# Four row blocks instead of two column halves: w_out's load and the order of batch 1's second layer in an attention and GELU kernel

## The chip, the core and the metric

The kernel runs on one core of a Trainium2 chip. Its time is the device time of one execution in microseconds; the number compared is the median of several runs. One further execution is recorded by the hardware profiler, and all rows below are from it. PE is TensorE, DVE is VectorE, ACT is ScalarE, POOL is GpSimd and SP is SyncE, which here only issues DMAs.

## What is computed

For 8 batches, 12 heads, 448 positions and a head width of 64, the reference normalizes q and k, computes attention, and puts the joined heads through two dense layers with a tanh GELU between them:

```python
q_n, k_n = rmsnorm(q, g_q), rmsnorm(k, g_k)
scores = (1 / sqrt(64)) * q_n @ k_n.T
attn = softmax(scores) @ v                          # 8 x 12 x 448 x 64
x = attn.transpose(0, 2, 1, 3).reshape(3584, 768)
h = x @ w_in                                        # 768 x 2048
out = gelu_tanh(h) @ w_out                          # 2048 x 768, out is 3584 x 768
```

Inputs and output are float32.

## The kernel before

The matmuls are in bf16. Batches are numbered from 0. The work is a pipeline over them: while the attention of batch b + 1 runs, the second layer of batch b is fed between its pieces. Everything is placed by hand. Each engine runs its instructions in the order in which the program emits them, and each queue issues its DMAs in that order too, so an instruction that waits holds up whatever was emitted behind it on its engine.

**Attention.** The 12 heads are three groups c = 0, 1, 2 of four heads. Within a group a `unit` (L321) is one of seven blocks t of keys: four PE matmuls of kT and qT into PSUM, then one exponential on ACT. `key_sums` (L340) adds the exponentials on DVE into `es`; `products` (L365) multiplies them by ones (sums) or V on PE; `turned` and `recips` make reciprocals on DVE, and `quad_x` writes xT, the first layer's input.

`attention` (L497) goes through eight groups of two or three units. Before each group the `side` steps of that number are emitted, after it the `behind` steps; in between a set number of second-layer steps are taken from the list `m2`, 20 in the first group of batch 1's attention and 13 in each of the next two, 96 in all.

**The second layer.** A step `mm2` (L432) is one matmul of 128 positions by 384 of w_out's 768 columns, for one block f of 128 of the 2048 hidden features. Sixteen steps, f = 0 to 15, fill one half of an output tile; then DVE, or ACT from the fourth group on in batch 1's attention, copies it into `osb`. After half 1 SP stores the whole tile in two DMAs. `m2_parts` (L482) lists the steps. The list made for b = 0 holds tiles 0 to 2 and runs during batch 1's attention; that is what the diff's title means by batch 1's second layer. It is sorted there by halves: half 0 of the three tiles, then half 1 of the three.

**Loads.** q and k are loaded by SP (`loads`; `late_loads` writes one element with DVE first, which holds the load until DVE has got there). Weights and V are loaded by POOL, which also squares and normalizes; these DMAs turn float32 into bf16 on the way. `w_in_part` loads half of w_in in four DMAs, `w_out_part` half of w_out's columns in one. They stand in the long step 8 of `mid` (L726), in this order: the second half of w_in, squares of batch 1's group 0, w_out half 0, batch 1's V, squares of group 1, w_out half 1.

**kT of group 1.** In batch 1's preparation kT and qT of groups 0 and 2 are transposed on PE, those of group 1 by DMA on SP (`dma_trans`, L308). `gain` (L316) then multiplies kT by the gains on DVE, emitted in group 1 of batch 1's attention ahead of that group's DVE work. The first unit that reads this kT is the second of the three in group 2. In the same two `side` groups batch 2's q and k are loaded (`late_loads` of its groups 0, then 1 and 2); POOL squares groups 0 and 1 and DVE sums the squares in `behind` of group 4.

Of the kernel before, what the change touches and what calls it, by code (L numbers as in the profile page):

```python
# [17 lines left out]
def kernel(  # L18
# [23 lines left out]
    HP = H // 2  # L42
    nf = d_ff // 128
    HD = d_model // 2
# [61 lines left out]
    wout = wts.tile([128, nf, d_model], BF16)  # L106
# [36 lines left out]
    def load_v(b, i, n):  # L143

        nc.gpsimd.dma_start(
            vb[b % 2][:, i:i + n].rearrange("p a t d -> p a (t d)"),
            v[b, 2 * i:2 * (i + n)].rearrange("(a r) (p t) d -> (r p) a (t d)", r=2, t=NT),
        )
# [6 lines left out]
    def square(b, c, n, eng, hs=both, ts=slice(0, NT)):  # L155
        if (n, b, c) not in sqs:
            sqs[n, b, c] = sqp.tile([P, 2, NT, D], F32, tag="sq", name="sq")
        sq, raw = squares(b, c, n, hs, ts), raws[n, b, c][:, hs, ts]
        if eng is nc.scalar:
            nc.scalar.activation(sq, raw, AF.Square)  # L160
        else:
            eng.tensor_mul(sq, raw, raw)  # L162
# [97 lines left out]
    def idle(n, w):  # L260

        for _ in range(n):
            nc.tensor.matmul(w, zeros[:, :128], zeros, start=True, stop=True)
# [168 lines left out]
    def mm2(b, i, half, f, lo, hi):  # L432

        end = b + 1 == B and i + 1 == 2 * S // 128
        if f == 0:
            osbs["ps"] = ps_m.tile([128, 512], F32, tag="mm", name="o")
            if lo == 0:
                osbs[i] = op.tile([128, d_model], F32, tag="osb", name="osb")
        o, osb = osbs["ps"][:, :hi - lo], osbs[i]
        nc.tensor.matmul(  # L440
            o, g[:, f, i * 128:(i + 1) * 128], wout[:, f, lo:hi],
            start=(f == 0), stop=(f == nf - 1),
        )
        if f + 1 < nf:
            return
        last = end and hi == d_model
        if b + 1 == B and (lo == 0 or end) or by_act:
            nc.scalar.copy(osb[:, lo:hi], o)  # L448
        else:
            nc.vector.tensor_copy(osb[:, lo:hi], o)  # L450
        if half == 0 and not end:
            return
        for j in range(2):
            col = i * 128 + j * R
            r = ((b // 2) * 2 + col // S) * R
            cols = slice(lo if end else 0, hi)
            eng = nc.scalar if last and j else nc.sync
            eng.dma_start(
                out_v[col % S // R, r:r + R, cols], osb[j * R:(j + 1) * R, cols]
            )  # L460
# [21 lines left out]
    def m2_parts(b):  # L482
        tiles = range(3) if b % 2 == 0 else range(3, 7)
        order = [(i, half) for i in tiles for half in range(2)]
        if b == 0:

            order.sort(key=lambda t: t[1])
        parts = [(i, half, half * HD, (half + 1) * HD) for i, half in order]
        if b + 1 == B:
            i, half, lo, hi = parts.pop()  # L490
            parts += [(i, half, lo, lo + HD // 2), (i, half, lo + HD // 2, hi)]
        return [
            lambda part=part, f=f: mm2(b, part[0], part[1], f, *part[2:])
            for part in parts for f in range(nf)
        ]
# [146 lines left out]

    def w_out_part(i):
        nc.gpsimd.dma_start(
            wout[:, :, i * HD:(i + 1) * HD],
            moe_w_out[:, i * HD:(i + 1) * HD].rearrange("(f p) d -> p f d", p=128),
        )

    def warm():
        return oall[0][:, :S]  # L650
# [57 lines left out]
    for a in range(2):  # L708
# [20 lines left out]
            lambda: normed(0, 2, "k", nc.vector, t_rest), lambda: recips(),  # L729
            lambda: w_in_part(1, 2),  # L730
            lambda: square(1, 0, "q", nc.gpsimd), lambda: square(1, 0, "k", nc.gpsimd),
            lambda: w_out_part(0), lambda: load_v(1, 0, HP),
            lambda: square(1, 1, "q", nc.gpsimd), lambda: square(1, 1, "k", nc.gpsimd),
            lambda: w_out_part(1)),
           (9, lambda: idle(2, warm())),
           (10, lambda: products(0, 0, 1, 0, 3)),
           (11, lambda: products(0, 0, 1, 3)),
# [24 lines left out]
    for b in range(B):  # L762
# [50 lines left out]
        for f in range(nf // 2 if b == 0 else nf):  # L813
# [7 lines left out]
            for fn in m1.get(f, ()):  # L821
                fn()
        m2 += m2_parts(b)
        if b + 1 == B:
            for fn in m2:
# [44 lines left out]
```

## Time and profile before

| | us |
|---|---|
| runs | 407.31, 406.19, 407.34; median 407.31 |
| profiled execution, time | 408.13 |
| its span | 406.4 |
| PE busy | 395.6 |
| ACT busy | 280.8 |
| DVE busy | 258.1 |
| POOL busy | 121.3 |
| w_out half 0, half 1: issued | 28.14, 33.47 |
| batch 1's V: issued | 29.36 |
| first second-layer matmul | 54.3 |

The span is the time from the first to the last instruction; the profiled execution's time is 1.7 us more. Times within the execution count from the start of the span. The second layer takes 912 matmuls of PE's 3331. The granted clock is 1.0 throughout.

### The profile page before, as it was taken

The page shows a single profiled execution, that of the slowest core. Times are in us where ns is not written, and L with a number is a line of the kernel's source. Part 1 is how long each engine was busy: PE and PEld are TensorE (multiplying, and loading weights), DVE is VectorE, ACT ScalarE, POOL GpSimd, SP SyncE. Part 2 cuts the span into 40 slices and gives each one's busy share as a digit, 9 for nine tenths or more (in the row PEclk, how much of TensorE's full clock was granted, in tenths as well). Part 3 has the DMA queues.
Part 4 walks back from the last instruction along what each step waited for, and adds up shares of the span by engine and source line. Part 5 has one row for each costly group of instructions (what it writes and reads, how often), then busy time and mean ns, then how long its engine had stood idle before and what let it go on. Part 6 is the DMA issues. An engine that isn't in the chain of part 4 may idle for free.

```text
span 406.4 us, 8105 instructions
## 1 busy us (share of the span) xinstructions
PE 395.6 (97%) x3331; PEld 209.4 (52%) x3331; DVE 258.1 (64%) x433; ACT 280.8 (69%) x380; POOL 121.3 (30%) x101
## 2 busy tenths in 40 slices
PE   7799999999999999999999999999999999999996
PEld 3354555555555555555555555555555555555564
DVE  4988956986698258945689357973598504990010
ACT  5995388967974888847976689748878349754301
POOL 4994307265005440092203640073300900000000
PEclk9999999999999999999999999999999999999999
DMA  8999996989613936159622939139713511111033
GB/s 268 322 209 207 200 188 230 233 192 260 107 40 86 271 54 185 39 123 286 122 65 48 235 82 227 43 73 255 98 40 80 111 27 39 42 48 31 1 78 78
DMA packets 65561, 54.07 MB, mean 133 GB/s; under 512 B 37364, under 2 KB 60532, under 8 KB 65524
## 3 DMA queue, kind: packets, MB, share of 16 engines
q1 hardware_dynamic: 53184, 41.48, 39.2%
q0 software_dynamic: 12112, 11.80, 18.7%
q8 instruction: 26, 0.43, 0.4%
q10 hardware_dynamic: 228, 0.28, 0.2%
q14 instruction: 11, 0.09, 0.1%
HBM read 45.61 MB, written 11.01 MB: 139 GB/s over the span
## 4 chain that ended last, share of the span: by engine, by line
PE 89%; DVE 3%; POOL 2%; DMA 2%; ACT 1%; issue 1%; SPq 0%; DVEq 0%; POOLq 0%
PE o L440 36%; PE h L419 23%; PE t L470 12%; PE t L330 9%; PE t L381 8%; DMA rawq<-in_q_dram 2%; ACT ex L334 1%; POOL g L162 1%; DVE st L390 1%; PE tp L288 1%; DVE rb L397 1%; POOL win L641 0%; DVE es L352 0%; DVE ss L167 0%; POOL sq L162 0%
## 5 line engine op out<-in xcount | busy, mean ns | idle before, releaser
L334 ACT ACTIVATE ex<-t,shift 128x896 bf16<-128x896 f32 x168 | 157.8, 1006 | 22.6 <-PE t L330 19.9
L440 PE MATMUL o<-wout,g 128*128 128x384 bf16 (+1 forms) x912 | 156.8, 324 | 0.0
L440 PEld LDWEIGHTS <-g 128*128 128x128 bf16 x912 | 83.6, 98 | 67.9 <-issue 18.9
L419 PE MATMUL h<-xT,win 128*128 128x448 bf16 x504 | 96.5, 352 | 0.0
L167 DVE TENSOR_REDUCE ss<-sq 128x14 f32<-128x896 f32 (+3 forms) x45 | 44.4, 1000 | 50.6 <-ACT sq L160 46.7
L419 PEld LDWEIGHTS <-win 128*128 128x128 bf16 x504 | 49.3, 98 | 46.0
L425 ACT ACTIVATE g<-h 128x448 bf16<-128x448 f32 x84 | 45.7, 544 | 28.1 <-PE h L419 23.0
L450 DVE COPY osb<-o 128x384 f32<-128x384 f32 x41 | 22.7, 554 | 52.4 <-PE o L440 50.5
L470 PE MATMUL t<-xT,win 128*128 128x448 bf16 x264 | 51.6, 352 | 0.1
L330 PE MATMUL t<-qT,kT 64*64 64x448 bf16 x672 | 47.0, 359 | 2.4 <-DVE kT L297 1.0
L475 ACT ACTIVATE g<-t 128x896 bf16<-128x896 f32 x22 | 19.4, 915 | 34.8 <-PE t L470 33.5
L654 POOL COPY mark<-es 1x1 bf16<-1x1 bf16 x6 | 1.1, 178 | 132.7 <-DVE es L352 132.7
L270 POOL TENSOR_TENSOR nrmq<-rawq,rinv 128x896 bf16<-128x896 f32 (+1 forms) x21 | 34.8, 1659 | 11.5 <-DVE o L233 7.3
L470 PEld LDWEIGHTS <-win 128*128 128x128 bf16 x264 | 25.7, 98 | 24.0 <-issue 0.8
L270 POOL TENSOR_TENSOR nrmk<-rawk,rinv 128x896 bf16<-128x896 f32 x19 | 31.9, 1681 | 0.0
L381 PE MATMUL t<-ex,vb 64*64 64x448 bf16 x588 | 31.6, 350 | 0.0
L330 PEld LDWEIGHTS <-kT 64*64 64x64 bf16 x672 | 17.2, 105 | 27.4 <-issue 20.3
L448 ACT COPY osb<-o 128x384 f32<-128x384 f32 (+1 forms) x16 | 7.3, 459 | 31.7 <-PE o L440 31.7
L162 POOL TENSOR_TENSOR sq<-rawq 128x896 f32<-128x896 f32 (+1 forms) x9 | 13.6, 1517 | 50.1 <-DVE ss L167 31.8
L397 DVE STREAM_TRANSPOSE rb<-rc 128x896 f32<-128x896 f32 x24 | 26.7, 1112 | 0.8
L390 DVE STREAM_TRANSPOSE st<-t 128x448 f32<-128x448 f32 x42 | 24.6, 625 | 3.2 <-PE t L381 3.1
L381 PEld LDWEIGHTS <-vb 64*64 64x64 bf16 x672 | 19.9, 107 | 12.4 <-issue 3.0
(89 smaller groups left out, 302.5 us busy)
## 6 DMA issues: line engine op xcount, KB each, us to landing
out_dram<-osb SPq DMA_DIRECT2D x54, 192.0 KB, 2.7
rawq<-in_q_dram SPq DMA_DIRECT2D x23, 448.0 KB, 4.6
rawk<-in_k_dram SPq DMA_DIRECT2D x23, 448.0 KB, 5.7
vb<-in_v_dram POOLq DMA_DIRECT2D x7, 672.0 KB, 6.7
win<-in_moe_w_in_dram POOLq DMA_DIRECT2D x8, 384.0 KB, 12.7
wout<-in_moe_w_out_dram POOLq DMA_DIRECT2D x2, 1536.0 KB, 23.9
vb<-in_v_dram POOLq DMA_DIRECT2D x1, 448.0 KB, 10.5
qT<-nrmq SPq DMA_TRANSPOSE x19, 5.0
```

Source lines behind the costliest of these rows:

```text
L167: nc.vector.reduce_sum(sss[b][:, c, "qk".index(n), hs, ts], squares(b, c, n, hs, ts), axis=AX.X)
L270: eng.tensor_mul(nrms[n, b, c][:, ts].rearrange("p t a d -> p a t d"), raws[n, b, c][:, :, ts], root[:, :, ts].to_broadcast([P, 2, m, D]),)
L330: nc.tensor.matmul(sc[r * R:(r + 1) * R, a, :S], kT[rs, c, t, r], qT[b][rs, c, :, r], start=True, stop=True,)
L334: nc.scalar.activation(ex[:, t], sc[:, :, :S], AF.Exp, scale=scale, bias=shift)
L381: nc.tensor.matmul(o[r][a * D:(a + 1) * D], vb[b % 2][rs, 2 * c + a, i] if what else ones[rs], es[i][rs, a], start=(i == 0), stop=(i == n ...
L390: nc.vector.transpose(st[:, r].rearrange("p a b -> p (a b)"), oas[0][r])
L397: nc.vector.transpose(rb.rearrange("p r s -> p (r s)"), rc.to_broadcast([128, 2 * S // 32, 32]))
L419: nc.tensor.matmul(h[:, :S], win[:, c, f * 128:(f + 1) * 128], xT[b][:, c], start=(c == 0), stop=(c == HP - 1),)
L425: nc.scalar.activation(g[:, f, (b % 2) * S:(b % 2 + 1) * S], h[:, :S], AF.Gelu_apprx_tanh)
L440: nc.tensor.matmul(o, g[:, f, i * 128:(i + 1) * 128], wout[:, f, lo:hi], start=(f == 0), stop=(f == nf - 1),)
L450: nc.vector.tensor_copy(osb[:, lo:hi], o)
L470: nc.tensor.matmul(h[:, j, :S], win[:, c, f * 128:(f + 1) * 128], xT[b][:, c], start=(c == 0), stop=(c == HP - 1),)
```

## The change

The two w_out loads, each of 2048 rows by 384 columns (rows of 1536 bytes in float32), become four loads of 512 rows by all 768 columns (3072 bytes). In the feature blocks that a matmul reads, load i holds f = 4i to 4i + 3, for both column halves. Two of them now stand ahead of the squares of group 1 and two behind them, and batch 1's V comes last. The sort by halves goes, so the list for b = 0 is tile 0 half 0, tile 0 half 1, tile 1 half 0 and so on, as for the other batches.

```diff
     def m2_parts(b):
         tiles = range(3) if b % 2 == 0 else range(3, 7)
         order = [(i, half) for i in tiles for half in range(2)]
-        if b == 0:
-
-            order.sort(key=lambda t: t[1])
...
     def w_out_part(i):
         nc.gpsimd.dma_start(
-            wout[:, :, i * HD:(i + 1) * HD],
-            moe_w_out[:, i * HD:(i + 1) * HD].rearrange("(f p) d -> p f d", p=128),
+            wout[:, 4 * i:4 * (i + 1)],
+            moe_w_out[512 * i:512 * (i + 1)].rearrange("(f p) d -> p f d", p=128),
         )
...
             lambda: w_in_part(1, 2),
             lambda: square(1, 0, "q", nc.gpsimd), lambda: square(1, 0, "k", nc.gpsimd),
-            lambda: w_out_part(0), lambda: load_v(1, 0, HP),
+            lambda: w_out_part(0), lambda: w_out_part(1),
             lambda: square(1, 1, "q", nc.gpsimd), lambda: square(1, 1, "k", nc.gpsimd),
-            lambda: w_out_part(1)),
+            lambda: w_out_part(2), lambda: w_out_part(3), lambda: load_v(1, 0, HP)),
```

## The prediction

> **What bounds the kernel now.** I read the page first (TensorE, PE, is busy 97% of the span), then the windows, to see whether it idles anywhere the change can reach. The columns of a row are PE, weight loads, DVE, ACT and POOL.
>
> ```profile
> 54.00:62.00 8.00, 8.00 (x70) 4.29 (x63) 4.39 (x14) 7.76 (x9) 0.00 (x0) 1.00 1.05 209
> 62.00:70.00 8.00, 8.00 (x95) 3.94 (x93) 4.74 (x7) 6.69 (x8) 6.47 (x6) 1.00 0.74 253
> 70.00:76.00 6.00, 6.00 (x70) 3.09 (x68) 5.84 (x12) 5.16 (x8) 1.29 (x2) 1.00 0.75 106
> 76.00:82.00 6.00, 6.00 (x83) 3.38 (x81) 5.40 (x10) 5.94 (x10) 2.93 (x3) 1.00 0.90 294
> ```
>
> The four rows cover batch 1's attention, in which the edited second layer runs. PE is full in all of them, and the later rows lose 0.16 us between 100 and 380. So no wait is there to be removed, and any wait put in front of PE after 54 us is added whole. The clock is 1.00 throughout.
>
> Next the landings, from the DMA view of narrow stretches; the last number is us from issue to landing.
>
> ```profile
> win<-in_moe_w_in_dram POOLq DMA_DIRECT2D x1, 384.0 KB, 16.2
> ...
> wout<-in_moe_w_out_dram POOLq DMA_DIRECT2D x1, 1536.0 KB, 19.6
> vb<-in_v_dram POOLq DMA_DIRECT2D x1, 672.0 KB, 22.7
> ...
> wout<-in_moe_w_out_dram POOLq DMA_DIRECT2D x1, 1536.0 KB, 28.2
> ...
> kT<-nrmk SPq DMA_TRANSPOSE x1, 13.4
> ```
>
> With the issue times of the timeline (24.22, 28.14, 29.36, 33.47, 45.34) they land at 40.4, 47.7, 52.1, 61.7 and 58.7: POOL's DMAs land in order of issue, one after the other. Half 0 of w_out is needed at 54.3 and half 1 at about 64.9, so neither is waited for now.
>
> Then the packets of both queues, in 40:42, 48:50 and 54:56 (q0 is POOL's queue, q1 SP's with the DMA transposes):
>
> ```profile
> q0 software_dynamic: 521, 0.40, 130.6%
> ...
> q0 software_dynamic: 374, 0.29, 91.5%
> q1 hardware_dynamic: 367, 0.09, 35.8%
> ...
> q0 software_dynamic: 372, 0.29, 90.7%
> q1 hardware_dynamic: 368, 0.09, 35.6%
> ```
>
> Alone, q0 moves 521 packets of 768 bytes in 2 us. Beside the transposes (256-byte packets) the two queues take turns one packet each, whatever the sizes. Last, the timeline around the place where kT lands:
>
> ```profile
> 54.27 3.42 PE L440 MATMUL o<-wout,g 128*128 128x384 bf16 x20
> 58.72 0.45 DVE L317 TENSOR_SCALAR kT<-kT,gcols 128x896 bf16<-128x896 bf16 x1 [0.55 <-DMA kT<-nrmk]
> 60.54 0.76 PE L330 MATMUL t<-qT,kT 64*64 64x448 bf16 x12
> 61.03 0.55 DVE L450 COPY osb<-o 128x384 f32<-128x384 f32 x1
> 61.64 0.37 SPq L122 DMA_DIRECT2D rawq<-in_q_dram  x1
> 77.66 1.35 DVE L352 TENSOR_TENSOR es<-es,ex 128x896 bf16<-128x896 bf16 x2
> 79.08 0.37 PE L381 MATMUL t<-es,ones 64*64 64x448 bf16 x4
> ```
>
> DVE already waits 0.55 us for kT, 2 us before PE reads it (the second of the three units at 60.54, so 60.8). At the end es is ready at 79.01 and read at 79.08: no slack there.
>
> **The change part by part.** The 96 second-layer steps, their evictions and the switch of evictions to ACT (a matter of the count alone) are the same: 0.
>
> *Issues on POOL.* A w_out half (2048 rows) takes 1.22 us, a part of w_in (192) 0.63: 0.32 us per 1000 rows, so a block of 512 is 0.73. Four are 2.93 instead of 2.43, hidden by POOL's idle 7.30 us before 41.98. The squares of (1, 1) start about 0.6 us earlier. V's issue goes from 29.36 to about 34.4; V is read at 66.3 and must land with the queue's end, about 61: 0.
>
> *The last w_out block.* V took 52.1 - 47.7 = 4.3 us in the queue and now comes last, so at an unchanged end w_out would be complete at 61.7 - 4.3 = 57.4. Three things make it earlier. Packets of 1536 bytes: from 61 ns at 768 (2 us x 16 engines / 521) and 157 ns at 2048 (204 in 30:32), 119 ns by interpolation, 3 ns saved on each of 128 per engine, 0.4. Transposes that have not yet got their turn: some 48 of 112 packets per engine, at 86 - 61 = 25 ns, 1.2. Batch 2's q loads, which shared the last 2.5 us before: about 0.9. So 54.9 to 57.4. The first tile reads block 3 at its 13th matmul, 54.34 + 12 x 0.168 = 56.4. PE waits 0 to 1.0; I take 0.3.
>
> *kT.* The two transposes, of qT and kT, move 458,752 bytes, 1792 packets or 112 per engine, each behind one of q0. Beside w_out a turn goes from 86 ns (32 us of 16 engines / 370) to 119 + 25 = 144 ns. Their first packets move at about 47.6 (DMA view in narrow windows). On an engine that began w_out at 37 (in 36:38 most packets are already of the small kind), 128 x 0.119 ends at 52.2 without them, with them at 53.2; 39 turns are done, 48 follow beside V at 91 ns (32 / 352), 25 alone, with the 0.4 us in which all packets stop near 53: kT lands at about 59.2. On the last engine (w_in's last landing is 40.4) the same sum ends at 61.8 and lands by 62.2. A landing is that of the last of 16 engines, so I stay near the upper end, and take the old end of all this traffic, 61.7, less the 0.4 saved: 61.2. The gain then ends at 61.7 instead of 59.2, and PE, which wants it at 60.8, waits 0.9 in all (the 0.3 above falls inside).
>
> The Trainium skill, "DMA: Bandwidth & Descriptors", section "Queues, rings and completion order", has engines alternate between queues by packets of typically 9 to 17 descriptors. The nearly equal counts above speak for one traced packet a turn. If turns were of about equal bytes, kT would still land at 58.7 and this term were 0.
>
> *What waits behind that gain.* On DVE: three additions, then the eviction that completes tile 0. That goes from 61.03 to about 63.5. SP now has tile 0's two stores (0.56 us each, from the pair at 107.44) ahead of batch 2's loads; with the halves those stores came at 74.1. So the loads go at about 65.2 instead of 61.64, 3.6 later. POOL's squares of (2, 1) end at 74.1 instead of 70.46. DVE's last reduction of them would start at 72.5 + 0.9 = 73.4: 0.7 late. DVE is packed from there to the es of 79.01, so PE waits 0.7 more. Without the late kT the stores cost 1.1 on SP, inside the 2.0 us of slack (72.5 - 70.46): 0.
>
> *Stores.* Two tiles leave earlier, out of SP's train of 9.28 us at 74.11. The next transposes wait for POOL's norms too, and PE is full from 82 to 100 (18.00 of 18.00): 0.
>
> Sum: 0.9 + 0.7 = +1.6, from 408.1 to 409.7 of the profiled execution. That one is 0.8 above the median of 407.3, so the median becomes 408.9. With kT at 62.7 the PE wait is 2.4 and the sum 3.1; with kT at 59.2 and block 3 at 56 it is 0.
>
> **The rivals.**
> 1. *All hidden.* The last engine catches up, or turns are by bytes; kT lands before 60.2. For it: 1.5 to 2 us of slack; an average engine is done at 59.2. Against: the 3.4 us by which the last engine trails. 407.3.
> 2. *Each smaller load costs a gap.* If every load pays about 2 us before the next moves, two more loads put w_out's end at 57 + 4 = 61, and PE waits 4.4 at its 13th matmul: 411.7. Against: the w_in parts land 1.6 to 2.4 us apart and are 393 KB each, about 200 GB/s, the rate of the long halves. The fixed 2.0 us per DMA are those of the Trainium skill, same page, section "Anatomy of one DMA — SWDGE (gpsimd) path"; this trace shows no such gap.
> 3. *Faster.* POOL squares 0.6 us earlier and leaves DVE alone sooner, while DVE makes the xT for which PE idles. It decides if the transposes and products at 30.4 to 36 become shorter. PE's idle time from 28 to 38 is 0.85 us (1.82, 1.47 and 1.86 busy of 2.00 in three rows), which with the 0.16 later bounds the gain at 1.0: 406.3. Against: DVE's pair of transposes takes 1.17 to 1.18 us beside POOL and without it.
>
> **How the numbers follow.** About 0.3% (1.2 us) is what a measurement of this kernel tells from no change. Forecast 0.60, of which 0.08 stays within 1.2 us; hidden 0.22; gap 0.10; faster 0.08, of which 0.05 passes the bound with the spread of the runs (406.19 to 407.34) and 0.03 does not. Slower 0.52 + 0.10 = 0.62; same 0.08 + 0.22 + 0.03 = 0.33; faster 0.05. The range takes in the hidden case with its spread, 406.6, and the forecast's upper cost 3.1 with half of the gap case, 411.2.
>
> **What would show it.** Right: DVE's idle time before the gain of kT grows from 0.55 to about 3 us, PE shows a wait of about 1 us at 60 to 62, batch 2's second loads are issued after 64 and tile 0's stores ahead of them. w_out's blocks land near 44, 48, 52 and 56. Wrong: PE still full from 54 to 82, or kT landed before 60; packets of q0 and q1 no longer equal in number while both run; or PE's wait at the 13th matmul is the larger one.

## The result and the profile after

The changed kernel takes 409.43 us (median of 20 runs, 407.44 to 411.89) against 406.81 (20 runs, 406.17 to 407.83) before: a ratio of 1.0067 [1.0053, 1.0081], or 2.6 us more. Its runs spread over 4.45 us, those of the kernel before over 1.66. The profiled execution took 408.96 us with a span of 407.2.

First the windows, on the same stretches as for the kernel before. The columns are PE, weight loads, DVE, ACT and POOL, then granted clock, DMA share and GB/s.

```profile
54.00:62.00 8.00, 7.72 (x65) 4.03 (x62) 2.88 (x8) 7.76 (x9) 0.00 (x0) 1.00 0.93 137
62.00:70.00 8.00, 8.00 (x95) 3.92 (x93) 5.76 (x13) 6.21 (x8) 3.54 (x3) 1.00 0.81 239
70.00:76.00 6.00, 5.64 (x67) 2.83 (x64) 5.42 (x12) 5.16 (x7) 4.21 (x5) 1.00 0.50 136
76.00:82.00 6.00, 6.00 (x84) 3.48 (x81) 5.53 (x9) 5.94 (x9) 2.12 (x3) 1.00 1.16 275
```

PE, full before in all four, now lacks 0.28 us in the first row and 0.36 in the third. DVE does 1.5 us less work in the first row (2.88 against 4.39) and 1.0 more in the second, and POOL's squares have moved from the second row (6.47 to 3.54) into the third (1.29 to 4.21). From the first matmul of L470 after this stretch (81.39 before, 82.19 after) to the end of the span both kernels take the same time, about 325.0 us. So the cost arises ahead of it.

The two queues in 48:50 and the landing of kT, from the DMA view:

```profile
q0 software_dynamic: 224, 0.34, 93.8%
q1 hardware_dynamic: 224, 0.06, 21.7%
...
kT<-nrmk SPq DMA_TRANSPOSE x1, 15.3
```

The two queues are still equal in packets, 224 each instead of 374 and 367. POOL's queue moves more bytes (0.34 MB instead of 0.29) and the transposes fewer (0.06 instead of 0.09). kT was issued at 45.02 and lands at 60.3. The blocks of w_out land at 42.7, 46.5, 50.8 and 55.4, V at 59.9. Now the timeline behind that landing:

```profile
60.37 0.45 DVE L317 TENSOR_SCALAR kT<-kT,gcols 128x896 bf16<-128x896 bf16 x1 [2.52 <-DMA kT<-nrmk]
60.88 0.57 PE L330 MATMUL t<-qT,kT 64*64 64x448 bf16 x8 [0.28 <-DVE kT L317]
62.66 0.55 DVE L450 COPY osb<-o 128x384 f32<-128x384 f32 x1
63.24 1.19 SPq L458 DMA_DIRECT2D out_dram<-osb  x2
64.52 0.55 SPq L122 DMA_DIRECT2D rawq<-in_q_dram  x1
69.78 1.83 POOL L162 TENSOR_TENSOR sq<-rawq 128x448 f32<-128x448 f32 x2 [3.48 <-DVE xT L405]
73.42 0.62 DVE L167 TENSOR_REDUCE ss<-sq 128x7 f32<-128x448 f32 x1 [0.27 <-POOL sq L162]
74.51 1.17 DVE L390 STREAM_TRANSPOSE st<-t 128x448 f32<-128x448 f32 x2
75.74 0.38 PE L330 MATMUL t<-qT,kT 64*64 64x448 bf16 x4 [0.36 <-DVE st L390]
```

Read it downwards. DVE idles 2.52 us for kT, and PE waits 0.28 for DVE's gain. The eviction of tile 0 comes at 62.66, its two stores go out, and only then q of batch 2's group 1 is issued, at 64.52 (before at 61.64). POOL starts its squares at 69.78 (before at 66.85), and though the row names xT as what ended the idle time, the q they need lands at 69.6, 5.1 us after the issue. DVE's sums of those squares, the last at 73.42, stand ahead of the transposition `st` of 74.51. That instruction empties the PSUM buffer which the last unit of group 5 writes to, and so PE waits a second time, 0.36 us at 75.74. In the kernel before, the same two places read as follows, and PE's twelve matmuls go through without a break:

```profile
73.70 1.18 DVE L390 STREAM_TRANSPOSE st<-t 128x448 f32<-128x448 f32 x2
74.66 0.76 PE L330 MATMUL t<-qT,kT 64*64 64x448 bf16 x12
```

### The profile page after: what moved, and what is told of

The parts are those of the page before. It is cut to its first block, busy times and chain, and to the rows that moved or that the text cites. A ratio compares the mean times of both kernels' runs of the same rounds, so it can differ in the third digit from the quotient of the medians.

```text
span 407.2 us, 8108 instructions
## 1 busy us (share of the span) xinstructions
PE 396.1 (97%) x3331; PEld 209.4 (51%) x3331; DVE 258.1 (63%) x433; ACT 280.8 (69%) x380; POOL 122.0 (30%) x103
## 4 chain that ended last, share of the span: by engine, by line
PE 81%; DVE 6%; DMA 6%; POOL 3%; issue 2%; ACT 1%; SPq 1%; DVEq 0%; POOLq 0%
PE o L440 33%; PE h L419 23%; PE t L470 8%; PE t L330 8%; PE t L381 7%; DMA kT<-nrmk 4%; DMA rawq<-in_q_dram 2%; DVE ss L167 1%; DVE st L390 1%; POOL sq L162 1%; PE o L381 1%; POOL g L162 1%; DVE rb L397 1%; DVE xT L410 1%; DVE es L352 0%
## 5 line engine op out<-in xcount | busy, mean ns | idle before, releaser
L167 DVE TENSOR_REDUCE ss<-sq 128x14 f32<-128x896 f32 (+3 forms) x45 | 44.6, 1000 | 50.8 <-ACT sq L160 45.9
L470 PE MATMUL t<-xT,win 128*128 128x448 bf16 x264 | 51.6, 352 | 0.1
L470 PEld LDWEIGHTS <-win 128*128 128x128 bf16 x264 | 25.7, 98 | 24.0 <-issue 0.8
```

The lines of the kernel that those rows point to most:

```text
L167: nc.vector.reduce_sum(sss[b][:, c, "qk".index(n), hs, ts], squares(b, c, n, hs, ts), axis=AX.X)
L470: nc.tensor.matmul(h[:, j, :S], win[:, c, f * 128:(f + 1) * 128], xT[b][:, c], start=(c == 0), stop=(c == HP - 1),)
```

## The experiments

Two theories for the size of the cost. One: the late kT alone makes it, by holding DVE and with it everything behind. The other: the stores, which now stand on SP ahead of batch 2's loads, must be there too. Beside them stood the rivals of the prediction. In the table, the first three columns come from timed runs, with the median of the kernel before on the same chip; the last five from the profiled execution: the first second-layer matmul, PE's waits for w_out, for group 1's kT or qT, and for `st`, and what is left of the time after that first matmul, less the 353.86 us that this is before (408.13 - 54.27). Each row has one profile, and the timed runs of a kernel spread around it.

| kernel | median (before) | ratio [95%] | start | w_out | kT, qT | `st` | cost |
|---|---|---|---|---|---|---|---|
| whole change, first profile | 409.43 (406.81) | 1.0067 [1.0053, 1.0081] | 53.95 | 0 | 0.28 | 0.36 | 1.15 |
| whole_again | 409.79 (407.03) | 1.0066 [1.0044, 1.0088] | 52.48 | 0 | 0.31 | 1.99 | 2.90 |
| whole_look | profile alone, 408.50 | | 53.05 | 0 | 0.35 | 0.78 | 1.59 |
| whole_look_2 | profile alone, 408.07 | | 53.56 | 0 | 0 | 0.36 | 0.65 |
| whole_look_3 | profile alone, 412.80 | | 54.14 | 0.38 | 1.52 | 2.14 | 4.80 |
| loads_only | 408.18 (406.47) | 1.0037 [1.0021, 1.0054] | 52.43 | 0 | 1.58 | 0 | 1.85 |
| order_only | 413.27 (406.47) | 1.0174 [1.0151, 1.0196] | 52.74 | 3.47 | 0 | 0 | 6.32 |
| v_last | 406.81 (406.47) | 1.0010 [0.9997, 1.0023] | 52.35 | 0 | 0 | 0 | 0.00 |
| v_late | 408.01 (406.47) | 1.0040 [1.0024, 1.0056] | 54.02 | 0.64 | 0 | 0 | 0.55 |
| loads_ahead | 407.85 (407.03) | 1.0019 [1.0002, 1.0036] | 53.81 | 0 | 0.36 | 0 | 0.53 |
| k_first | 407.55 (407.03) | 1.0009 [0.9987, 1.0031] | 54.12 | 0 | 0.84 | 0 | 0.64 |
| stores_behind | 408.42 (406.59) | 1.0030 [1.0012, 1.0049] | 53.39 | 0.22 | 1.54 | 0 | 2.24 |
| k_first_loads_ahead | 408.04 (406.59) | 1.0021 [1.0004, 1.0039] | 52.47 | 1.40 | 0.09 | 0 | 1.47 |

The start varies by 1.7 us between the five executions of the whole change, but in every profile, that of before included, it comes 26.13 or 26.14 us after the issue of the first w_out load. What moves it lies before the first edited instruction, and the last column leaves it out.

**Each half of the change alone.** loads_only keeps the new loads and puts the sort back; order_only takes the sort out and keeps the old loads.

```diff
 # loads_only: the four blocks, V last, and in m2_parts again
+        if b == 0:
+            order.sort(key=lambda t: t[1])
 # order_only: no sort, w_out by column halves, V behind half 0
```

> The four row blocks with V last, but the second layer still by halves (the order of before). Theory 1 (kT of group 1 is late because the transposes take turns with packets twice as large; the late gain and, behind it, tile 0's stores ahead of batch 2's loads make PE wait): kT lands at 59.5 to 62 as after the whole change, DVE's idle time before the gain is 2 us or more, PE waits for it, but SP issues batch 2's second loads at about 63, right behind their DVE writes, without the stores, so the second wait (DVE's sums behind POOL's squares, 0.4 to 0.7 us) is gone. Time 0.5 to 2 us above before, less than the 2.6 of the whole change. Theory 2 (the order by tiles is the cost: the stores stand ahead of the loads, the late kT is within its slack): time as before within 0.5 us. Theory 3 (w_out itself lands late for the tile order): as before, since half 1 is then read only from 64.9.

> The second layer tile by tile, with the loads of before (two column halves, V between them). Half 1 of w_out lands at about 61.7 and is now read at the 17th matmul, 54.3 + 16 x 0.168 = 57.0. Both theories 1 and 3: PE waits 4.7 us there for the DMA of w_out, kT lands at about 58.7 inside that wait and costs nothing of its own; time 4 to 5.5 us above before. Theory 2 (order by stores alone): about 2.6 us above, as with the whole change, with no PE wait at the 17th matmul.

loads_only costs 0.37%, a little over half of the whole. Its DMA view of 48:50, and PE's wait in its timeline:

```profile
q0 software_dynamic: 227, 0.34, 93.9%
q1 hardware_dynamic: 224, 0.06, 21.6%
...
kT<-nrmk SPq DMA_TRANSPOSE x1, 16.6
```

```profile
60.66 0.57 PE L330 MATMUL t<-qT,kT 64*64 64x448 bf16 x8 [1.58 <-DVE kT L317]
```

kT lands 16.6 us after its issue, at 60.1, and that one wait, 1.58 us, is most of its cost of 1.85. There is no second wait. So the new loads alone make kT late, and the new order adds something else.

order_only cost more than twice what the whole change does, 6.8 us by the medians, above the 4 to 5.5 expected. From its timeline, and its windows:

```profile
58.98 1.46 PE L440 MATMUL o<-wout,g 128*128 128x384 bf16 x4 [3.47 <-DMA wout<-in_moe_w_out_dram]
```

```profile
55.00:59.00 4.00, 0.53 (x5) 0.12 (x3) 1.55 (x5) 1.41 (x2) 0.00 (x0) 0.84 1.11 201
59.00:61.00 2.00, 2.00 (x12) 0.77 (x16) 0.00 (x0) 0.00 (x0) 0.11 (x1) 0.50 0.82 265
```

The 17th matmul, the first of half 1, waits 3.47 us for the second load. Then the granted clock falls to 0.50; it is 0.50 until 63 and 0.61 from 63 to 65, and thirteen second-layer matmuls take 3.71 us instead of 2.29. PE is busy throughout these six microseconds, so the low clock loses 1.0 + 1.0 + 0.8 us of work there; with the wait that is 6.3, the cost of this profile (6.32). The waits of up to 2.14 us in whole_look_3 left it at 1.00. The Trainium skill, "TensorE: Matmul & The Clock Gate", section "What's actually happening", has the clock fall to half after an idle window of about 3.4 us; this trace agrees, with 3.47 us. So the sort by halves was what hid the second load before; in tile order with column halves it is waited for.

**V moved, the packets kept.** v_last takes the kernel before and moves one issue only.

```diff
-            lambda: w_out_part(0), lambda: load_v(1, 0, HP),
+            lambda: w_out_part(0),
             lambda: square(1, 1, "q", nc.gpsimd), lambda: square(1, 1, "k", nc.gpsimd),
-            lambda: w_out_part(1)),
+            lambda: w_out_part(1), lambda: load_v(1, 0, HP)),
```

> Before with one move alone: batch 1's V issued behind w_out half 1; column halves (packets of 768 bytes) and the order by halves stay. It differs from the run with row blocks and order by halves only in the size of w_out's packets and the place of two issues. Theory 1 (turns by packet): the transposes still pass one for each 768-byte packet, at some 86 ns a turn, and kT lands at 58.2 to 59, as before; no PE wait; time as before within 0.4 us. Rival (kT is late because V now stands last in the queue and the queue as a whole ends at 60 to 61, whatever the packets): kT lands at 60 to 61 and the time is 0.5 to 2 us above before, equal to the row blocks with order by halves.

The ratio's interval includes 1, and PE shows no wait. This profile and that of loads_only start alike, at 52.35 and 52.43, so they compare directly. From the DMA views of v_last, the packets in 48:50 and kT's line in 46:48, and then its gain:

```profile
q0 software_dynamic: 372, 0.29, 90.7%
q1 hardware_dynamic: 372, 0.10, 36.0%
...
kT<-nrmk SPq DMA_TRANSPOSE x1, 13.2
```

```profile
56.61 0.45 DVE L317 TENSOR_SCALAR kT<-kT,gcols 128x896 bf16<-128x896 bf16 x1 [0.37 <-DMA kT<-nrmk]
```

The queue ends at the same time in both (V lands at 60.1 here, at 59.9 in loads_only), with the same bytes in the same order of weights and V. Yet kT lands at 56.6 with packets of 768 bytes and at 60.1 with those of 1536. The counts of the two queues are equal in both, 372 to 372 and 227 to 224, while the bytes are not. What delays kT is neither V's place nor the end of the queue, but the size of the packets that it takes turns with. (The two kernels also differ in the number of w_out loads, four for two, and by 0.7 us in the issue of V; no run separates these from the size.)

**V taken out of the competition.** v_late is the whole change, but POOL issues V only when batch 1's first sums of exponentials are there, at about 57.7.

```diff
-            lambda: w_out_part(2), lambda: w_out_part(3), lambda: load_v(1, 0, HP)),
+            lambda: w_out_part(2), lambda: w_out_part(3)),
...
-            side += [(1, lambda: late_loads(2, 0), lambda: gain(1, 1)),
+            side += [(1, lambda: gpsimd_waits(ess[1, 0][:1, 0, :1]), lambda: load_v(1, 0, HP),
+                      lambda: late_loads(2, 0), lambda: gain(1, 1)),
```

> The whole change, but batch 1's V is issued by POOL only when batch 1's first key sums are there (about 57), so that the transposes of group 1 meet w_out's packets and nothing after them. Theory 1: the transposes run alone once w_out has landed (55.4 on the last engine) and kT lands at 56.5 to 58.5, before DVE gets to the gain or shortly after; PE waits for it no more; stores cost 1.1 us on SP inside the slack; V lands at about 64.5, before 66.5, when it is read. Time as before within 0.6 us, that is some 2 us below the whole change, and the spread of its runs falls from 4.5 us towards that of before, 1.7. Theory 2 (stores ahead of loads): time as with the whole change, 2 to 2.6 us above before. If V comes too late (after 66.5) PE waits there for it, and the time says nothing of kT.

DVE no longer idles ahead of the gain (58.13), and PE's only wait is 0.64 us for w_out's last block, at its 13th second-layer matmul. So in this profile a kT in time takes both later waits away. At 1.0040 it still isn't as fast as before: its median is 1.5 us above, where 0.6 was expected and the profile costs 0.55. The late last block is one candidate for the rest. V is another: it lands at 66.5, and its first weights are read at 66.7, so a slightly later V would be waited for. Which of them it is in the timed runs is not shown.

**The whole change again, and batch 2's loads put first.** loads_ahead moves the loads of batch 2's groups 1 and 2 one step earlier on SP and DVE, ahead of the gain and of tile 0's stores.

```diff
-            side += [(1, lambda: late_loads(2, 0), lambda: gain(1, 1)),
-                     (2, lambda: late_loads(2, 1), lambda: late_loads(2, 2))]
+            side += [(1, lambda: late_loads(2, 0), lambda: late_loads(2, 1),
+                      lambda: late_loads(2, 2), lambda: gain(1, 1))]
```

> The whole change once more, for a second profile. In the runs so far kT lands at 57 to 60 by the DMA stream, while the first second-layer matmul starts anywhere from 52.3 to 54.3, so the profiled run of the change (53.95) would be one in which PE came late. Theory 1: with a start near 52.4 PE waits 1.5 to 2 us for the gain of kT, its time is then 409 to 410; with a start near 54 it waits 0.3. In both, POOL's squares of (2, 1) end late and DVE and then PE wait 0.4 to 1 more. Theory 2 (only the stores ahead of the loads cost): no wait for kT however early PE is.

> The whole change, with batch 2's second and third q and k loads (and the DVE writes that hold them) moved ahead of the gain of kT, so neither the gain nor tile 0's stores stand before them. Theory 1: the wait for kT stays (0.3 to 2 us of PE by the start), the second wait behind POOL's squares goes; time 1 to 2 us above before, as with row blocks in the order by halves (1.7). Theory 2 (the stores are the whole cost): time as before within 0.4 us. If the second wait has another cause: 2.6 us above, as the whole change.

> The whole change, a third profile for the relation between when PE comes and how long it waits for kT: by theory 1 the wait is the landing of kT plus 0.6 us (gain and its signal) less the time at which PE comes to the second unit of group 2 (6.5 us after the first second-layer matmul), and nothing where that is negative.

The repeat gave the same ratio, and whole_look a second wait of 0.78 us between the others. In whole_again that wait was 1.99 us, in spite of a kT wait like that of the first profile. Expected were 1.5 to 2 us for kT from a start of 52.48, but kT landed earlier as well, at 58.9, and PE waited 0.31. Three lines of its timeline:

```profile
60.27 1.84 POOL L162 TENSOR_TENSOR sq<-rawq 128x896 f32<-128x896 f32 x1 [16.75 <-DMA rawq<-in_q_dram]
60.67 1.91 DVE L352 TENSOR_TENSOR es<-es,ex 128x896 bf16<-128x896 bf16 x1
76.03 0.38 PE L330 MATMUL t<-qT,kT 64*64 64x448 bf16 x4 [1.99 <-DVE st L390]
```

The third addition behind the gain takes 1.91 us beside POOL's square of 1.84, and holds up tile 0's eviction; in the first profile POOL began later and the addition took 0.62. In the five profiles of the whole change it took about 1.9 in those with a second wait of 2.0 and 2.1, and 0.62 or 0.63 in the three others. The Trainium skill, "SBUF — State Buffer", section "Who interferes with whom", says that a DVE instruction with two SBUF inputs contends with a GpSimd instruction that reads SBUF, the later one being blocked for the whole of it. The trace agrees: the addition began 0.40 us after POOL's square, ended 0.47 after it, and took 1.91 instead of 0.62.

loads_ahead issues batch 2's loads at 61.03. The second wait is gone, the first is not:

```profile
60.82 0.57 PE L330 MATMUL t<-qT,kT 64*64 64x448 bf16 x8 [0.36 <-DVE kT L317]
```

The ratio falls from 1.0066 to 1.0019 on the same chip.

**The stores, or the gain?** loads_ahead passes both. stores_behind passes only the stores: tile 0's two stores are issued by SP after the loads, which stay behind the gain.

```diff
+        def store():
...                                  # the loop over the two store DMAs, as before
+        if (b, i) == (0, 0):
+            held.append(store)       # tile 0: put off
+        else:
+            store()
...
-                     (2, lambda: late_loads(2, 1), lambda: late_loads(2, 2))]
+                     (2, lambda: late_loads(2, 1), lambda: late_loads(2, 2),
+                      lambda: held.pop()())]
```

> The whole change, with tile 0's two stores emitted on SP behind batch 2's second and third q and k loads instead of ahead of them; the gain of kT stays ahead of those loads' DVE writes. In the profiles of the whole change the second wait (DVE's transposition of the sums behind POOL's squares of (2, 1)) is 0.4, 2.0 and 0.8 us, the wait for kT 0.3 to 0.4. Theory A (the stores cost, by standing ahead of the loads on SP and in its DMA queue): the loads go 1.2 us earlier and land 2 us or more earlier, the second wait goes, and the time is 0.3 to 1.2 us above before, like the run with the loads ahead of both (0.8). Theory B (the late gain costs, by holding up additions, eviction and the loads' DVE writes): the second wait stays at 0.3 us or more and the time is 1.5 to 2.5 us above before.

```profile
61.97 0.57 PE L330 MATMUL t<-qT,kT 64*64 64x448 bf16 x8 [1.54 <-DVE kT L317]
65.64 0.37 SPq L122 DMA_DIRECT2D rawq<-in_q_dram  x1
```

This execution had a late kT (61.4) and issued the loads at 65.64, later than the 64.52 of the whole change, with an addition of 1.92 as well. Still the second wait is gone: the q so issued lands in 3.2 us, at 68.9, where with the stores ahead it takes 5.1 (first profile), 5.6 (whole_again) and 5.7 us (whole_look_3). The landing also depends on what else is in SP's queue: before, without stores, this q took 5.1 us, but it was issued only 3 us behind group 0's k. The fair pair is whole_again and loads_only, which start alike, issue group 0's k at 56.89 and 56.84 and this q at 64.37 and 64.33, with the stores ahead and without them. From their DMA views:

```profile
rawq<-in_q_dram SPq DMA_DIRECT2D x1, 448.0 KB, 5.6
rawq<-in_q_dram SPq DMA_DIRECT2D x1, 448.0 KB, 3.2
```

In this pair the stores cost 2.4 us by standing in the queue, and 1.19 by their issue.

This settles the second wait: without the stores ahead of the loads, even a later gain does not cause it (loads_only, with a 1.58 us wait and its loads at 64.33, says the same). PE itself comes 1.5 us later in these two, which gives DVE room, but whole_look_3 has the same wait for kT (1.52), the same late gain (8.2 us after the start, here 8.1) and the same slow addition, with the stores ahead, and there the second wait is 2.14. What is left of the cost, 2.24 in this profile, is the wait for kT and that for w_out. By its time, 1.8 us above before, the run falls into the range given for theory B; it is the trace that speaks against B. Why loads_ahead is only 0.8 above is not shown by the waits of the two profiles; the intervals of the two ratios overlap.

**kT first.** k_first lets POOL normalize k before q and SP transpose kT before qT; k_first_loads_ahead adds the edit of loads_ahead.

```diff
-                   lambda: rsqrt_newton(1), lambda: normed_both(1, 1, nc.gpsimd),
+                   lambda: rsqrt_newton(1), lambda: normed(1, 1, "k", nc.gpsimd),
+                   lambda: normed(1, 1, "q", nc.gpsimd),
...
-                  (4, lambda: transposed(1, 1)),
+                  (4, lambda: dma_trans(1, 1, "k"), lambda: dma_trans(1, 1, "q")),
```

> The whole change, but of group 1's two DMA transposes kT goes first and qT second (POOL normalizes k first too). The gain needs kT alone, so it is done while qT is under way, at 55 to 57, and holds up nothing on DVE; PE then waits for qT at 60 to 61 where it waited for the gain. Theory 1: PE's wait at the second unit of group 2 stays but is 0.5 us shorter (no gain between the landing and PE), tile 0's eviction comes some 1 to 2 us earlier and the second wait goes; time 0.8 to 1.8 us above before. Rival (it is the gain on DVE and what is behind it that costs, not PE's own need of group 1's transposes): time as before within 0.4 us.

> The whole change, with kT's transpose ahead of qT's and batch 2's loads ahead of the gain and the stores. What is left is PE's own need of the later of the two transposes. If the two costs are those two waits and nothing else: time 0 to 0.8 us above before (0.3 to 0.5 for the wait at qT), no second wait. If w_out's larger packets or POOL's moved issues cost something of their own: 1 us or more above before.

In k_first the gain finds kT there (57.94) and DVE does not wait. PE now waits for qT itself, which lands at 61.5 (16.3 us after 45.19):

```profile
61.60 0.57 PE L330 MATMUL t<-qT,kT 64*64 64x448 bf16 x8 [0.84 <-DVE rawk L140]
```

The row names a DVE write of rawk, but that was done at 58.0, and the landing of qT fits. The profiled execution took 408.62, 1.1 us more than the median. At 1.0009 [0.9987, 1.0031] it is the only version of the change that can't be told from the kernel before; none is faster. With the loads ahead as well, PE lost 0.09 us to qT (landed at 60.6), but only because it had waited 1.40 us for the last w_out block before. The median is 1.45 us above before, outside the 0 to 0.8 expected if the two waits were all: the last w_out block is a third. The intervals of the two ratios overlap, so the second edit shows no gain on top of the first.

**Two more profiles of the whole change.**

> The whole change, a fourth profile. By both theories the wait for kT and the second wait add up to its time above an execution of before with the same start of the second layer; one with a time above 410 would show a second wait above 2 us.

> The whole change, a fifth profile, for the same relation: the wait for kT plus the second wait against the time, with the start of the second layer taken off.

They mark the two ends. In whole_look_2 PE waits 0.36 us in all. In whole_look_3 everything is late: 0.38 us for w_out, 1.52 for kT and 2.14 for `st`.

Over the five profiles the costs are 0.65 to 4.80 us, mean 2.2 (1.15 + 2.90 + 1.59 + 0.65 + 4.80, by 5); the timed runs say 2.6. PE's waits are 1.7 of that mean. A wait that breaks a group of twelve attention matmuls into eight and four costs another 0.19 (0.57 + 0.38 against 0.76 in the rows), once or twice in each profile; 0.1 to 0.4 us remains that no row names.

## Why the prediction was right, and where its sizes were off

The forecast was slower by 1.6 us, at 408.9; measured are 2.6 and 409.4, inside the range. That the two times lie so close is in part luck: 408.9 started from a median of three runs, 407.3, and that of twenty is 406.8. Within the sum, too, errors cancel: over the five profiles kT cost 0.5 and not 0.9, the wait behind it 1.1 and not 0.7. Point by point:

*PE is full, so waits count whole.* It held: time after the start less waits is 354.15 to 354.62 in the five profiles, against 353.86.

*Issues on POOL, 0.73 us a block: 0.* A pair of blocks takes 1.55 or 1.56, V is issued at 34.18 (forecast 34.4), and POOL idles 6.63 us ahead of its next work. Nothing waits for it.

*The last w_out block, 0.3.* It landed at 55.4, inside 54.9 to 57.4. PE waited 0 in four profiles and 0.38 in the fifth. v_late and k_first_loads_ahead show up to 1.40, above the bound of 1.0.

*kT, 0.9.* The mechanism held: equal numbers of packets from both queues, a turn of 143 ns beside w_out (32 us of 16 engines by 224) where 144 was forecast, and a landing at 60.3 where 61.2 was forecast. It was tested by v_last against loads_only. The landing was forecast 0.9 us too late, of which 0.3 is the earlier start of that execution, and so the term was mis-sized: PE waited 0 to 0.35 in four profiles and 1.52 in one, 0.5 in the mean. With turns of equal bytes kT would have stayed where it was, so for these packets the reading from the counts decides. Equal counts do not tell whether a turn is one packet of each queue or several of each; the sum needs only their equality. The 204 packets that the working takes from 30:32 stand in 32:34 (221 less 17 small ones); with the 196 of 30:32 a packet of 1536 bytes would be 122 ns and not 119, which changes little. The sign given for an error, a kT landed before 60, was badly put: it landed at 58.9 to 59.5 in three profiles, but those had started 0.7 to 1.8 us earlier than the profile before. Counted from the first second-layer matmul it lands 5.8 to 8.2 us later, against 4.4 before.

*Behind the gain, 0.7.* This is the term that was too small: 0.36, 0.36, 0.78, 1.99 and 2.14, mean 1.1. The chain was as forecast up to POOL and DVE's sums (additions, eviction, stores, loads, squares, and the last sum at 73.42 where 73.4 was forecast). Its door into PE was another: not es at 79, but the PSUM buffer that `st` frees at about 75.7. What the sum left out is above all the third addition, which takes 1.9 us instead of 0.62 where POOL squares beside it: the two profiles with it have the 1.99 and 2.14, the three others 0.5 in the mean, less than the 0.7. The time that the stores occupy the queue of the loads was not in the sum by name. It went in by luck: the sum moved the landings with the issues, that is at the 5.1 us of before, and behind the stores they took 5.1 to 5.7, where 3.2 would have been enough without them. That the stores without a late kT cost nothing fits k_first and v_late, which have them and no second wait.

*Rivals.* All hidden: refuted, since kT does come late, though whole_look_2 shows it nearly hidden at 0.65. A gap for each load: refuted, blocks of 768 KB in bf16 land 3.8 to 4.6 us apart, which leaves no room for 2 us at the 200 GB/s of these stretches, and the queue ends at 59.9, before at 61.7. Faster: refuted. From the issue of the first w_out load to the first second-layer matmul, the stretch in which it had to arise, both kernels take 26.13 us.

What stays open: why the landings differ between executions of one kernel. No view here shows the 16 DMA engines one by one, and no run separates what holds a landing up. The cost of the whole change varies from 0.65 to 4.80 between the profiles.

## What to carry to other kernels

Where two DMA queues take turns by packets, making the packets of one larger slows the other, here kT by 3.5 us, though no byte was added and the queue ends no later. Before changing the shape of a load, look at what else moves at that time and who waits for it. When an order brings a store forward, ask which loads stand behind it in the same queue, in bytes as well as in issue time. If a cost hangs on a race between a landing and an engine, one profile is not its size: five profiles here gave 0.65 to 4.80 us.

## What was not expected of the hardware

The granted clock fell to 0.50 after a PE wait of 3.47 us and stayed at 0.84 or below in the rows from 55 to 65, which turned that wait into 6.3 us of time in that profile; waits of up to 2.14 us had no such effect. A landing in SP's queue took 5.6 us behind two stores and 3.2 without them, issued at the same time. A bf16 addition of 128x896 on DVE went from 0.62 to 1.91 us beside a POOL multiplication of 1.84, longer than POOL's instruction itself.
